# A retention and channel-mix kernel: blocks 4 and 5 in 64-token chunks, block 8 turned by transfers, and another written order

## The chip, the core and the metric

The kernel runs on one core of a Trainium2 chip, as one launch. The metric is the time of that launch on the device, in microseconds; less is better. Before the change it is 153.48 us (median of 3 runs, 153.37 to 153.55).

## What is computed

Four sequences of 768 tokens with 8 heads of 64 go through a recurrent retention: each head holds a 64 x 64 state that decays by its own factor and adds k v at each token, and the output is q times the state. The output (512 features a token) goes through a channel mix: each token is blended with the one before it, and two blends feed a squared-ReLU pair of products (512 to 1024 to 512) and a sigmoid gate.

```python
for t in range(S):
    state = gamma * state + einsum('bhd,bhe->bhde', k[:, :, t], v[:, :, t])
    y[:, :, t] = scale * einsum('bhd,bhde->bhe', q[:, :, t], state)
...
xk = mu_k * x + (1.0 - mu_k) * x_prev
xr = mu_r * x + (1.0 - mu_r) * x_prev
k = np.maximum(xk @ w_k, 0.0)
v = k * k @ w_v
r = 1.0 / (1.0 + np.exp(-(xr @ w_r)))
return (r * v).astype(np.float32)
```

Inputs and output are float32; the products run on float16.

## The kernel before

The 3072 tokens are cut into 12 blocks of 256, numbered 0 to 11, three to a sequence. A block's work is a row of steps, and each step is one function:

- `lq`, `lk`, `lv`: POOL issues transfers that bring the block's queries, keys and values into rings of four buffers, queries and keys as float16. `vs` (L291, VectorE) scales the values by the decays.
- `Tq`, `Tk`: TensorE turns queries and keys so that features lie on the partitions, and `Eq`, `Ek` (L276, ScalarE) copy them out of PSUM. A block in `PAIRQ` or `PAIRK` is turned by eight 128 x 128 transposes (L348) each, a block in neither list but in `HALF` by 32 transposes of 64 x 64 (L343), the others by L354. Blocks in `DT` are not turned by TensorE: SyncE issues a transposing transfer instead (`tq`, `tk`, L388).
- `S`: scores within a chunk. `M` (L457, VectorE): the causal mask. A block in `WIDE` has two chunks of 128 tokens, whose scores fill 128 x 2048 (L425), so it has two masks. A block in `HALF` has four chunks of 64, with half as many scores (L412) and one mask. Blocks 0 and 1 are in a third form (L433).
- `C`: the products of keys and values that carry the state from chunk to chunk (L487 wide, L469 half). `U` (L522): the sums of these, two for a wide block and four for a half one. `G`: the decay into the next block (L527 on ScalarE, L531 on VectorE).
- `I`, `J` (L544): queries times the carried state; `Y`: masked scores times values (L590 wide, L574 half; in a half block the second part of L544 follows within `Y`). `sy` is a small copy that orders the two.
- `D`: the eviction of the retention output with its scale (L640 in one piece, L633 in two for a half block). `dx` (L655): the difference from the token before. `X` (L681): the two blends, one instruction for each of four feature groups, `X.n.0.j` for the keys' blend and `X.n.1.j` for the gate's.
- `K` (L695 for a pair of blocks, L705 for one): the key products of the channel mix; `Qa`, `Qb` (L727, L741, L745; ScalarE): ReLU and square. `R` (L754) and `s` (L760): the gate and its sigmoid. `V` (L766): the value products, in two halves. `O` (L772, VectorE): the gated result; `st`: its store, issued by SyncE.

Blocks 3 and 4, 6 and 7, 9 and 10 go through `dx`, `X` and `K` as pairs, under the number of the first. `z` are products of zeros that fill TensorE while it waits at the start.

The order of all steps is written out by hand as words in one string: `S.6@67` is the score step of block 6 into PSUM banks 6 and 7, `Eq.6~a` runs on ScalarE (`v` VectorE, `p` POOL, `s` SyncE). The program is emitted word by word, and each engine runs its own words in that order; semaphores make it wait for what it needs from other engines. A bank or a buffer is used again once its last reader is done, so the bank numbers set waits too.

Of the kernel before, what the change touches and what calls it, by code (L numbers as in the profile page):

```python
# [44 lines left out]
Qb.1.2~a Tq.3@0 D.2~v R.1.1@7 s.1.0 Eq.3~a wv.0~p C.3@23 dx.2~v Tk.3@4 U.3.0~a R.0.0@5 lq.7~p
Ek.3~a U.3.1 X.2.0.1 Tk.4@2 wv.1~p X.2.0.3 s.0.1 S.3.0@01 X.2.0.2 S.3.1@34 s.0.0 lk.5~p X.2.0.0
Tq.4@6 s.1.1 M.3.0 K.2.1@5 Eq.4~a K.2.3@7 M.3.1 lq.5~p Qa.2.1~a Ek.4~a K.2.0@6 X.2.1.1 vs.4~v
Qa.2.3~a I.3@45 lv.5~p S.4.1@23 Qa.2.0~a S.4.0@01 K.2.2@7 G.3~a M.4.1 Y.3 Qb.2.0~a M.4.0 C.4@23
Qb.2.3~a V.0.1.0@6 Qa.2.2~a U.4.0~v J.3 Qb.2.2~a U.4.1 I.4@01 Y.4 sy.4~a D.3~v Qb.2.1~a lq.6~p
Tq.7@23 Qb.1.3~a J.4 V.1.1.0@7 X.2.1.3 G.4~a D.4~v V.0.0.0@4 Eq.7~a lv.7~p V.0.1.1 dx.4~v  # L50
V.1.0.0@5 dx.3~v V.0.0.1 X.2.1.0 lv.8~p V.2.1.0@2 X.3.0.0 X.3.0.1 Tk.5@3 V.1.1.1 X.2.1.2 Ek.5~a
lv.6~p X.3.0.2 V.1.0.1 X.3.0.3 Tq.5@3 X.3.1.1 K.3.5@0 lk.7~p O.0.1 V.2.1.1 O.1.1 X.3.1.2 K.3.1@1
O.1.0 K.3.2@7 lk.6~p Qa.3.1~a X.3.1.3 Eq.5~a K.3.3@5 vs.5~v Qa.3.5~a R.2.1@1 O.0.0 Qa.3.3~a
K.3.0@0 vs.7~v st.0.0 s.2.1 st.0.1 Qb.3.3~a K.3.6@3 st.1.1 X.3.1.0 Qa.3.0~a st.1.0 lv.11~p
Qa.3.2~a S.5.1@45 vs.6~v S.5.0@01 Qb.3.5~a C.5@6 K.3.4@7 Qb.3.1~a U.5.0~v lv.10~p M.5.0 Qa.3.6~a
R.3.0@6 Qb.3.0~a Qa.3.4~a R.2.0@3 M.5.1 s.3.0 lv.9~p Tq.6@01 s.2.0 I.5@67 O.2.1 Tk.6@45 sy.5~a
Eq.6~a Y.5 lq.8~p Tk.7@23 Qb.3.2~a J.5 R.3.1@0 D.5~v lq.11~p Qb.3.4~a V.2.0.0@1 Ek.7~a dx.5~v
V.2.0.1 s.3.1 Qb.3.6~a K.3.7@0 X.5.1.2 Ek.6~a lk.8~p X.5.0.1 V.3.0.0@2 vs.8~v Qa.3.7~a C.6@45
Qb.3.7~a X.5.1.1 S.6@67 lq.9~p X.5.0.2 V.3.1.0@0 U.6.0~a U.6.1 V.4.0.0@3 U.6.2 O.2.0 lq.10~p
V.3.0.1 M.6 st.2.0 R.4.0@1 U.6.3 X.5.1.0 S.7@45 s.4.0 O.3.0 I.6@67 V.4.0.1 sy.6~a G.6~a M.7 st.3.0  # L60
Tq.8@12 Y.6 X.5.1.3 Eq.8~a C.7@45 X.5.0.0 V.3.1.1 U.7.0~v lk.11~p X.5.0.3 R.5.0@1 U.7.1 U.7.2
K.5.1@2 U.7.3 lk.10~p s.5.0 D.6~v K.5.0@4 V.4.1.0@1 G.7~v Qa.5.0~a lk.9~p O.4.0 Qa.5.1~a I.7@45
O.3.1 C.8@67 sy.7~a Tk.8@23 dx.6~v st.3.1 Y.7 Ek.8~a st.2.1 V.4.1.1 D.7~v K.5.2@0 R.5.1@2 dx.7~v
Qa.5.2~a Qb.5.0~a K.5.3@3 s.5.1 X.6.0.3 R.4.1@0 Qb.5.1~a X.6.0.1 Qb.5.2~a V.5.0.0@2 tk.9~s X.6.0.2
Qa.5.3~a X.6.0.0 V.5.1.0@4 Qb.5.3~a s.4.1 vs.10~v tq.9~s K.6.4@3 K.6.7@0 X.6.1.3 Qa.6.4~a tq.10~s
X.6.1.1 V.5.0.1 Qa.6.7~a O.4.1 K.6.1@3 X.6.1.2 K.6.6@5 U.8.0~v Qa.6.1~a U.8.1 Qb.6.7~a V.5.1.1
vs.9~v K.6.2@3 U.8.2 O.5.1 I.8@67 S.8@01 Qa.6.2~a X.6.1.0 K.6.0@4 tk.11~s Qb.6.2~a M.8 Qa.6.6~a
R.6.0@3 Qa.6.0~a O.5.0 Y.8 s.6.0 S.9@45 st.5.0 Qb.6.6~a D.8~v C.9@01 st.4.1 R.7.1@3 tk.10~s
Qb.6.1~a Qb.6.0~a K.6.3@2 dx.8~v tq.11~s R.6.1@6 Qa.6.3~a X.8.1.0 s.7.1 K.6.5@7 X.8.1.3 Qb.6.3~a
st.4.0 X.8.0.1 st.5.1 R.7.0@3 Qb.6.4~a X.8.0.2 X.8.0.0 Qa.6.5~a V.7.0.0@2 X.8.0.3 U.9.0~a s.7.0  # L70
U.9.1 K.8.3@7 vs.11~v Qb.6.5~a K.8.0@3 Qa.8.3~a M.9 V.7.0.1 Qa.8.0~a X.8.1.1 K.8.2@7 Qb.8.0~a
U.9.2 U.9.3 V.6.1.0@3 O.7.0 Qa.8.2~a s.6.1 G.9~v st.7.0 C.10@01 S.10@45 Qb.8.2~a U.10.0~v I.9@67
K.8.1@2 sy.9~a M.10 V.6.1.1 Qa.8.1~a U.10.1 Qb.8.3~a U.10.2 V.6.0.0@4 U.10.3 Qb.8.1~a O.6.1
I.10@01 Y.9 sy.10~a X.8.1.2 C.11@23 G.10~v Y.10 D.9~v V.8.0.0@5 V.8.0.1 D.10~v R.8.1@6 dx.9~v
# [865 lines left out]
```

## Time and profile before

| | |
|---|---|
| median of 3 runs | 153.48 us |
| the profiled execution | 153.66 us |
| its span, first to last instruction | 151.8 us |
| TensorE matmuls busy | 143.5 us (95%) |
| VectorE busy | 127.6 us (84%) |
| ScalarE busy | 92.9 us (61%) |
| POOL busy | 62.0 us (41%) |
| granted TensorE clock | 1.000 |
| bytes read and written | 24.31 MB and 6.29 MB |

The profile is of one execution; its times are in microseconds. Rows of groups read: line, engine, operation, output and inputs with their shapes, count, then total and mean (ns) and the idle time ahead of the group with what ended it. Rows of a timeline and of the chain begin with the start and the length. In the rows of waits stand the total, the number and the longest. PE is TensorE, PEld its weight loads, DVE VectorE, ACT ScalarE, SP SyncE. The products of a row overlap, so the chain, which counts each stretch of time once, tells better than the mean of one what a product costs. Rows of the program's order carry no time.

### The profile page before, as it was taken

To read this page: it belongs to the slowest core of one execution; us is meant where nothing else is said; L and a number is where in the kernel's file an instruction comes from. 1 tells how busy PE (TensorE), PEld (TensorE's weight loads), DVE (VectorE), ACT (ScalarE), POOL (GpSimd) and SP (SyncE) were. 2 spreads that over 40 slices of the span, in tenths; PEclk is the share of its full clock that TensorE was granted. 3 is DMA by queue.
4 is the path that set the end of the run, shared out by engine and by line. 5 is a ranking of instruction groups with operands and counts; after the bars stand their busy time and mean duration, and the time that the engine had idled before them with its cause. 6 is when DMAs were issued, how large, how long until landed. Compare 5 with 4: busy or idle time off the path is not lost.

```text
span 151.8 us, 4947 instructions
## 1 busy us (share of the span) xinstructions
PE 143.5 (95%) x2125; PEld 82.6 (54%) x2125; DVE 127.6 (84%) x204; ACT 92.9 (61%) x179; POOL 62.0 (41%) x77
## 2 busy tenths in 40 slices
PE   7888789999999999999989999999999999999991
PEld 3355458757864544555457634546664444546650
DVE  2289799999999999969979999999899995399141
ACT  3665724998986229996435664778741078931860
POOL 7974678999549852997558000000000000000000
PEclk9999999999999999999999999999999999999999
DMA  4999999999999999999999947369200035000404
GB/s 137 245 236 190 181 244 242 162 171 210 196 175 239 226 208 196 322 221 186 161 219 142 210 85 139 67 178 246 73 4 0 4 140 207 0 4 29 179 33 174
DMA packets 56525, 23.83 MB, mean 157 GB/s; under 512 B 48056, under 2 KB 52024, under 8 KB 56504
## 3 DMA queue, kind: packets, MB, share of 16 engines
q0 software_dynamic: 45200, 14.95, 83.2%
q1 hardware_dynamic: 10872, 8.26, 18.1%
q8 instruction: 16, 0.26, 0.8%
q10 hardware_dynamic: 432, 0.32, 0.7%
q14 instruction: 5, 0.04, 0.1%
HBM read 24.31 MB, written 6.29 MB: 202 GB/s over the span
## 4 chain that ended last, share of the span: by engine, by line
PE 72%; DVE 10%; DMA 6%; ACT 4%; POOL 3%; issue 2%; DVEq 0%; POOLq 0%
PE ps L766 24%; PE ps L695 14%; PE ps L754 11%; PE ps L705 9%; DMA q<-in_q_dram 6%; DVE xk L681 2%; PE ps L348 2%; PE ps L544 2%; ACT k2s L745 2%; ACT kr L727 2%; PE ps L590 2%; PE ps L425 2%; DVE dx L655 2%; DVE a L457 2%; DVE xT L633 1%
## 5 line engine op out<-in xcount | busy, mean ns | idle before, releaser
L766 PE MATMUL ps<-wv,k2s 128*128 128x512 f16 x184 | 43.7, 379 | 0.0
L727 ACT ACTIVATE kr<-ps 128x512 f32<-128x512 f32 x48 | 27.6, 599 | 22.0 <-PE ps L705 12.0
L766 PEld LDWEIGHTS <-k2s 128*128 128x128 f16 x184 | 17.4, 98 | 19.3
L457 DVE TENSOR_TENSOR a<-ps,c_sb 128x1024 f16<-128x1024 f32 (+1 forms) x20 | 21.7, 1109 | 4.0 <-PE ps L412 3.2
L754 PE MATMUL ps<-wr,xr 128*128 128x512 f16 x96 | 24.0, 380 | 0.0
L760 ACT ACTIVATE rs<-ps 128x512 f32<-128x512 f32 x24 | 13.9, 598 | 15.9 <-PE ps L754 6.6
L695 PE MATMUL ps<-xk,wk 128*128 128x512 f16 x96 | 22.7, 379 | 0.1
L705 PE MATMUL ps<-xk,wk 128*128 128x256 f16 x192 | 22.8, 273 | 0.0
L270 POOL DMA_DIRECT2D v<-in_v_dram x20 | 17.9, 901 | 9.2 <-DVE vs L291 3.9
L705 PEld LDWEIGHTS <-wk 128*128 128x128 f16 x192 | 18.4, 98 | 3.7
L681 DVE SCALAR_TENSOR_TENSOR xr<-dx,mu,xT 128x256 f16<-128x256 f32 (+1 forms) x36 | 19.8, 566 | 0.1
L772 DVE SCALAR_TENSOR_TENSOR os<-ps,rs 128x512 f32<-128x512 f32 x23 | 15.3, 681 | 5.4 <-ACT rs L760 5.3
L270 POOL DMA_DIRECT2D k<-in_k_dram x20 | 17.6, 899 | 5.3 <-PE ps L469 3.1
L681 DVE SCALAR_TENSOR_TENSOR xk<-dx,mu,xT 128x256 f16<-128x256 f32 (+1 forms) x36 | 18.7, 567 | 0.1
L291 DVE TENSOR_TENSOR vs<-v,csm_sb 128x1024 f16<-128x1024 f32 x12 | 14.6, 1216 | 2.9 <-DMA v<-in_v_dram 2.9
L695 PEld LDWEIGHTS <-wk 128*128 128x128 f16 x96 | 9.1, 97 | 11.1 <-DVE xk L681 0.6
L655 DVE TENSOR_TENSOR dx<-xT 128x1024 f32<-128x1024 f32 x12 | 14.5, 1221 | 0.2
L741 ACT ACTIVATE k2s<-kr 128x512 f16<-128x512 f32 x24 | 14.5, 632 | 0.1
L745 ACT ACTIVATE k2s<-kr 128x512 f16<-128x512 f32 x24 | 14.1, 628 | 0.2
L754 PEld LDWEIGHTS <-xr 128*128 128x128 f16 x96 | 8.9, 98 | 9.3 <-DVE xr L681 0.2
L276 ACT COPY kT<-ps 128x1024 f16<-128x1024 f16 (+1 forms) x10 | 9.3, 930 | 7.1 <-PE ps L348 3.4
L270 POOL DMA_DIRECT2D q<-in_q_dram x12 | 10.7, 904 | 1.5 <-DMA v<-in_v_dram 0.7
(74 smaller groups left out, 150.4 us busy)
## 6 DMA issues: line engine op xcount, KB each, us to landing
out_dram<-os SPq DMA_DIRECT2D x23, 256.0 KB, 2.4
v<-in_v_dram POOLq DMA_DIRECT2D x20, 256.0 KB, 7.4
k<-in_k_dram POOLq DMA_DIRECT2D x21, 128.0 KB, 6.3
q<-in_q_dram POOLq DMA_DIRECT2D x13, 128.0 KB, 7.7
q<-in_q_dram POOLq DMA_DIRECT2D x5, 256.0 KB, 8.9
v<-in_v_dram POOLq DMA_DIRECT2D x2, 512.0 KB, 6.8
wv<-in_moe_w_v_dram POOLq DMA_DIRECT2D x2, 512.0 KB, 9.5
wk<-in_moe_w_k_dram POOLq DMA_DIRECT2D x2, 256.0 KB, 9.2
```

What stands on the lines that cost most here:

```text
L270: e.dma_start(out=to[:, i, hs], in_=src[:, i])
L291: e.tensor_tensor(out=VS(n), in0=V32(n).rearrange("p (h i d) -> p i h d", i=2, h=H), in1=gks[:, int(half(n) or wide(n)), :, :, None].to_br ...
L457: nc.vector.tensor_tensor(out=dst, in0=dst if n in SPLITM else src, in1=mask[:, None, None, :].to_broadcast(list(dst.shape)), op=ALU.mult,)
L655: e.tensor_tensor(out=DX(k)[:, :, m * TM + t0 : m * TM + t1], in0=x[:, :, c + t0 : c + t1], in1=x[:, :, c - 1 + t0 : c - 1 + t1], op=ALU.s ...
L681: nc.vector.scalar_tensor_tensor(out=XM[w](k)[:, j, t0:t1], in0=DX(k)[:, j, t0:t1], scalar=mu[:, w * NCO + j : w * NCO + j + 1], in1=x[:, ...
L695: nc.tensor.matmul(banks("K", n, g), lhsT=wk16[:, co, g * P : g * P + P], rhs=XM[0](k)[:, co, :], start=(co == 0), stop=(co == NCO - 1),)
L705: nc.tensor.matmul(pz[:, i, :], lhsT=wk16[:, co, fo * P : fo * P + P], rhs=XM[0](k)[:, co, m * TM + t0 : m * TM + t1], start=(i == 0 and c ...
L727: nc.scalar.activation(out=kr, in_=banks("K", n, g, *u), func=AF.Relu)
L745: nc.scalar.activation(out=K2(n)[:, w * g : w * g + w, t0:t1], in_=kr.rearrange("p a t -> p (a t)").rearrange("p (i t) -> p i t", i=w), fu ...
L754: nc.tensor.matmul(banks("R", n, tb), lhsT=XM[1](k)[:, co, t : t + P], rhs=wr16[:, co, :], start=(co == 0), stop=(co == NCO - 1),)
L766: nc.tensor.matmul(banks("V", n, tb), lhsT=K2(n)[:, fo, tb * P : tb * P + P], rhs=wv16[:, fo, :], start=(fo == 0), stop=(fo == NFO - 1),)
L772: nc.vector.scalar_tensor_tensor(out=OS(2 * n + tb), in0=banks("V", n, tb), scalar=1.0 / (KSC * KSC), in1=RS(2 * n + tb), op0=ALU.mult, op ...
```

## The change

Blocks 4 and 5 leave `WIDE`, `PAIRQ` and `PAIRK` and enter `HALF`: they are computed in 64-token chunks and turned by 64 x 64 transposes. Block 8 enters `PAIRQ` and `PAIRK` and the list of blocks turned by transposing transfers, which is now one list for queries and one for keys with the same members. Ahead of the first score products the order of words is the same but for one bank; behind them all of it is a new order, with other banks. Of that string the lines around block 1's scores are shown.

```diff
-HALF = (6, 7, 8, 9, 10, 11)
+HALF = (4, 5, 6, 7, 8, 9, 10, 11)
...
-PAIRQ = (3, 4, 5, 9, 10, 11)
-PAIRK = (3, 4, 5, 9, 10, 11)
-WIDE = (2, 3, 4, 5)
+PAIRQ = (3, 8, 9, 10, 11)
+PAIRK = (3, 8, 9, 10, 11)
+WIDE = (2, 3)
...
-DT = (9, 10, 11)
+DTQ = (8, 9, 10, 11)
+DTK = (8, 9, 10, 11)
...
-M.0.0.2.4 vs.1~v wk.0~p z.4@6 Y.0 Tk.1@2 D.0~v mt@3 C.1@45 me Ek.1~a Tq.1@3 U.1.0~v dx.0~v Tq.2@0
-Eq.1~a U.1.1 z.1@1 S.1.1@23 Eq.2~a I.1@67 X.0.0.1 S.1.0@45 lv.2~p M.1.1 G.1~a M.1.0 wr~p X.0.0.0
+M.0.0.2.4 vs.1~v wk.0~p z.4@6 Y.0 mt@0 Tk.1@1 D.0~v me C.1@45 Ek.1~a Tq.1@0 U.1.0~v dx.0~v Eq.1~a
+U.1.1 z.3@7 I.1@01 S.1.1@23 X.0.0.3 Tq.2@4 M.1.1 S.1.0@67 lv.2~p Eq.2~a M.1.0 wr~p X.0.0.0 z.5@5
...
     def laid(t, n):

-        if n in DT:
+        if n in (DTK if t is KT else DTQ):
             return t(n).rearrange("c j i p -> c (j i) p").rearrange("c (i j) p -> c j i p", j=NJ)
         return t(n)
```

More of the change, by code (lines that the diff above doesn't have):

```diff
@@ L45 @@
[L45 to L74, printed above, removed]
@@ L81 @@
[L81 to L85 removed]
+Tq.0.0.2@0 ck.0.0.2~a lq.1~p Eq.0.0.2~a lq.2~p z.3@7 Tk.0.0.2@1 Ek.0.0.2~a wk.1~p gy.1~a z.3@7
@@ new lines @@
+G.3~a Tk.4@67 M.3.0 I.3@23 K.2.3@1 sy.3~a Ek.4~a X.2.1.1 Y.3 Qa.2.2~a C.4@67 J.3 S.4@45 Qa.2.3~a
+U.4.0~v V.1.1.0@0 D.3~v Qb.2.2~a Qb.2.0~a V.0.0.0@1 lq.6~p X.2.1.0 Qb.2.3~a U.4.1 V.0.1.0@2
+Qb.2.1~a X.2.1.3 U.4.2 V.1.0.0@3 M.4 V.0.0.1 U.4.3 dx.3~v Tq.7@67 I.4@45 V.0.1.1 lq.11~p sy.4~a
+O.0.0 Y.4 st.0.0 O.0.1 V.1.0.1 D.4~v lk.6~p st.0.1 R.2.0@2 O.1.0 V.1.1.1 s.2.0 lk.7~p dx.4~v
+Eq.7~a V.2.0.0@1 O.1.1 Tk.5@23 Tq.5@67 lv.6~p X.3.0.0 Tq.6@45 R.2.1@0 X.3.0.3 Eq.6~a X.3.0.2
+V.2.0.1 Ek.5~a lv.7~p X.3.0.1 V.2.1.0@4 G.4~a vs.5~v V.2.1.1 Eq.5~a X.3.1.3 K.3.7@5 lq.10~p s.2.1
@@ new lines @@
+O.2.0 K.3.6@6 O.2.1 Qa.3.7~a X.3.1.2 C.5@01 st.2.1 Qa.3.6~a S.5@45 st.1.1 U.5.0~v Tk.6@23 st.1.0
+X.3.1.0 K.3.2@6 Ek.6~a X.3.1.1 K.3.0@7 Qb.3.7~a U.5.1 vs.6~v K.3.3@2 Qa.3.0~a Qb.3.6~a R.4.0@3
+U.5.2 lv.10~p Qa.3.3~a M.5 K.3.5@7 s.4.0 Qa.3.2~a vs.7~v I.5@23 S.6@45 lv.8~p sy.5~a C.6@01 Y.5
+M.6 U.6.0~a Qb.3.2~a K.3.4@6 Qb.3.0~a lv.9~p D.5~v R.4.1@4 Qa.3.4~a Qb.3.3~a K.3.1@5 U.6.1
+Qa.3.5~a dx.5~v lk.9~p R.3.1@2 Qa.3.1~a R.3.0@3 Qb.3.1~a U.6.2 X.5.0.0 s.3.1 lk.8~p V.3.0.0@5
+X.5.1.3 s.3.0 X.5.0.3 s.4.1 U.6.3 I.6@23 C.7@67 X.5.0.2 sy.6~a Tk.7@01 X.5.0.1 Y.6 lq.8~p vs.8~v
@@ L86 @@
+O.11.0 Vc.11.1.1@0 st.11.0 Oc.11.1.0 sc.11.1.0~s Oc.11.1.1 sc.11.1.1~a
 """
```

53 lines of the change are left out of this document (34 added, 19 removed).

## The prediction

> **What bounds the kernel now.** I read the page first, then the busy times by stage, then TensorE's waits, and last the chain and the timelines of single engines.
>
> The head of the page (busy time and share of the span), then the shares of the chain that ended last:
>
> ```profile
> span 151.8 us, 4947 instructions
> PE 143.5 (95%) x2125; PEld 82.6 (54%) x2125; DVE 127.6 (84%) x204; ACT 92.9 (61%) x179; POOL 62.0 (41%) x77
> ```
>
> ```profile
> PE 72%; DVE 10%; DMA 6%; ACT 4%; POOL 3%; issue 2%; DVEq 0%; POOLq 0%
> ```
>
> The stages (columns: length, then busy time of PE, PEld, DVE, ACT, POOL):
>
> ```profile
> 20.00:64.00 44.00, 43.47 (x564) 27.72 (x567) 43.72 (x63) 31.85 (x61) 32.92 (x39) 1.00 1.55 215
> 64.00:90.00 26.00, 25.40 (x559) 14.76 (x544) 23.57 (x38) 16.59 (x32) 14.41 (x17) 1.00 1.58 177
> 90.00:149.00 59.00, 58.60 (x751) 31.76 (x748) 47.03 (x78) 33.29 (x63) 0.00 (x0) 1.00 0.33 93
> ```
>
> TensorE is full from 20 us to its end, just short of 149 us. VectorE is full too, but only up to 90 us. So the end is the sum of TensorE's work and its waits, and until 90 us VectorE can become the bound at once. The waits of TensorE after 20 us:
>
> ```profile
> PE ps L574 <- issue: 0.5, 1, 0.5
> ...
> PE ps L590 <- ACT seen_y L276: 0.3, 1, 0.3
> PE ps L425 <- DVE xT L640: 0.2, 1, 0.2
> ```
>
> and, in the list of all engines' waits, one of the weight loads:
>
> ```profile
> PEld L695 <- DVE xk L681: 0.6, 1, 0.6
> ```
>
> That is 1.6 us. The last is that of the first key product of blocks 6 and 7 (K.6.4) for its mixed tokens; in the chain it starts here:
>
> ```profile
> 89.40 1.90 PE ps L695 x8
> ```
>
> **The change, part by part.**
>
> *TensorE's work.* The chain gives each group's time free of overlap. A block in 128-token chunks (turning, scores, state, scores times values, carried state):
>
> ```profile
> 32.81 0.24 PE ps L544 x8
> ...
> 36.25 0.45 PE ps L348 x8
> 36.70 0.55 PE ps L425 x16
> ...
> 42.19 0.57 PE ps L590 x16
> 42.76 0.25 PE ps L487 x16
> 43.01 0.97 PE ps L766 x4
> ...
> 54.23 0.86 PE ps L766 x4
> ```
>
> A block in 64-token chunks, same steps:
>
> ```profile
> 64.25 0.27 PE ps L343 x32
> ...
> 97.97 0.38 PE ps L574 x32
> 98.34 0.15 PE ps L544 x14
> 98.49 0.30 PE ps L412 x32
> 98.80 0.27 PE ps L469 x32
> ```
>
> Turning and carried state happen twice a block. Wide: 0.90 + 0.55 + 0.25 + 0.57 + 0.48 = 2.75 us. Half: 0.54 + 0.30 + 0.27 + 0.38 + 0.30 = 1.79 us. Blocks 4 and 5 save 2 x 0.96 = 1.9 us, and block 8 gives up two turnings, 0.54 us. Together **-2.45 us**, all on the path, since nothing else shortens a full engine.
>
> A switch between full-size products and small ones has a price: the four products (L766) behind a small group take 0.97 us in the rows above, elsewhere 0.86. The new order has 22 such switches from Y.1 on, the old one 20, because blocks 4 and 5 were turned by full-size transposes (L348) and are now turned in 64 x 64 tiles: **+0.2 us**.
>
> The Trainium skill, "TensorEngine Tiling (Array Packing)", Key Properties, speaks against the change here: every change of the tiling mode drains the engine. The weight loads show such a stop of 0.42 us:
>
> ```profile
> 34.39 0.33 PEld L487 LDWEIGHTS <-k 128*64 128x64 f16 x16 [0.42 <-issue]
> ```
>
> By that rule, with a full 0.42 us lost on the path at each, the two switches would cost 0.8 instead of 0.2 us; the 0.11 us between the two rows of L766 says that most of it is hidden, and I keep that.
>
> *VectorE's work.*
>
> ```profile
> L457 DVE TENSOR_TENSOR a<-ps,c_sb 128x1024 f16<-128x1024 f32 x16 | 19.1, 1215 | 4.0 <-PE ps L412 3.2 <-PE ps L433 0.8
> L522 DVE TENSOR_TENSOR tg<-ps,tg 128x256 f16<-128x256 f32 x20 | 8.4, 418 | 1.4 <-PE ps L469 1.2
> L633 DVE TENSOR_TENSOR xT<-ps,gy_sb 128x512 f32<-128x512 f32 x12 | 8.3, 690 | 2.2 <-PE ps L544 1.3
> L640 DVE TENSOR_TENSOR xT<-ps,gy_sb 128x1024 f32<-128x1024 f32 x6 | 7.3, 1220 | 1.3 <-ACT qT L276 1.1
> ```
>
> Two maskings go (-2.43), four state sums come (+1.67), two whole evictions of the retention output become four halves (+0.32): -0.44 us. So VectorE loses a fifth of what TensorE loses.
>
> *The start.* In the list of order the turning of block 2's queries (Tq.2) moves from ahead of block 1's scores (S.1.1) to between them.
>
> ```profile
> 16.05 0.79 PE L354 MATMUL ps<-c_sb,q 128*64 128x128 f16 x16 [1.20 <-DMA q<-in_q_dram]
> ...
> 17.09 0.42 PE L433 MATMUL ps<-qT,kT 64*64 64x128 f16 x16
> ...
> 31.60 0.31 PE L544 MATMUL ps<-qT,tg 64*64 64x128 f16 x8
> ```
>
> ```profile
> 14.91 1.03 ACT L276 COPY qT<-ps 128x1024 f16<-128x1024 f16 x1
> ```
>
> ```profile
> 16.36 0.47 DVE L681 SCALAR_TENSOR_TENSOR xk<-dx,mu,xT 128x256 f16<-128x256 f32 x1
> 17.63 2.36 DVE L457 TENSOR_TENSOR a<-ps,c_sb 128x1024 f16<-128x1024 f32 x2 [0.80 <-PE ps L433]
> ```
>
> S.1.1 needs ScalarE's copy, done at 15.94, not the transfer that lands at 16.0. It can start 1.1 us sooner; the masks (L457) then start when VectorE is free, 16.83 instead of 17.63, so **-0.8 us**. It is at most 1.1 and at least 0, should a later load hold the next step.
>
> *ScalarE and SyncE.* Block 8 gives up two evictions, each like the copy above (1.03 us), and gets two transfers instead:
>
> ```profile
> kT<-k SPq DMA_TRANSPOSE x3, 3.2
> qT<-q SPq DMA_TRANSPOSE x3, 3.2
> ```
>
> ScalarE loses 2.1 us, but is 61% busy; I count nothing. The transfers stand on SyncE's queue behind the stores of block 3 and ahead of those of block 4. Block 8's loads are issued, by the count of loads below, twelve issues of 0.9 us behind vs.6 (some 61.5 us), and land 7.1 to 11.1 us later, at 79 to 83 us; the two transfers then end by 90. Its scores come four groups into blocks 6 and 7, about 92 us. If that cover went, TensorE would wait for the excess. Behind the transfers wait the stores of blocks 4 and 5, whose tiles come up for reuse only with the results of blocks 6 and 7: nothing.
>
> *New waits.* Two masks took 2.36, so they follow each other at 1.14; short mixes (L681) follow at 0.40. With such spacings I went along the new order, engine by engine, to the places where one needs another.
>
> VectorE's row around block 2's second masks as it was (a_2 masked scores, tg_2_95 the first sum of its state, vs_76 its scaled values, xr_105 block 1's gate mixes; the first masks stand ahead of these rows):
>
> ```order
> L291 TENSOR_TENSOR vs_76<-v_2_72,csm_sb 128x1024
> L681 SCALAR_TENSOR_TENSOR xr_104<-dx_99,mu,xT_130 128x256
> L681 SCALAR_TENSOR_TENSOR xr_105<-dx_100,mu,xT_130 128x256 x2
> L522 TENSOR_TENSOR tg_2_95<-ps,tg_2_89 128x256
> L457 TENSOR_TENSOR a_2_85<-ps,c_sb 128x1024
> L291 TENSOR_TENSOR vs_74<-v_3_73,csm_sb 128x1024
> ```
>
> The same place on VectorE now:
>
> ```order
> L291 TENSOR_TENSOR vs_76<-v_2_72,csm_sb 128x1024
> L681 SCALAR_TENSOR_TENSOR xr_105<-dx_100,mu,xT_130 128x256 x2
> L457 TENSOR_TENSOR a_2_85<-ps,c_sb 128x1024
> L522 TENSOR_TENSOR tg_2_95<-ps,tg_2_89 128x256
> L681 SCALAR_TENSOR_TENSOR xr_105<-dx_100,mu,xT_130 128x256
> L291 TENSOR_TENSOR vs_74<-v_3_73,csm_sb 128x1024
> ```
>
> Both masks now stand ahead of the sum, for which block 2's inter product (I.2) waits. From 16.83 VectorE does five masks and value scalings (5.7), D.1 and dx.1 (2.3) and 13 mixes (5.2), then the sum (0.34): 30.4 us. TensorE started I.2 at 31.60; now one gate group less (0.86) stands ahead of it, and it comes 0.8 sooner, so it gets there at 29.9: a wait of 0.5 us (0 to 1).
>
> ScalarE's row around block 4's keys (kT_81 their copy, qT_78 that of its queries, tg_1_88 the state carried into block 4) as it was:
>
> ```order
> L276 COPY qT_78<-ps 128x1024
> L727 ACTIVATE kr_110<-ps 128x512
> L276 COPY kT_81<-ps 128x1024
> L727 ACTIVATE kr_107<-ps 128x512
> L727 ACTIVATE kr_108<-ps 128x512
> L527 ACTIVATE tg_1_88<-t_0_86,csm_sb 128x64 x4
> ```
>
> The same place on ScalarE now:
>
> ```order
> L276 COPY qT_78<-ps 128x2x4x128
> L727 ACTIVATE kr_109<-ps 128x512
> L745 ACTIVATE k2s<-kr_107 128x512
> L727 ACTIVATE kr_110<-ps 128x512
> L527 ACTIVATE tg_1_88<-t_0_86,csm_sb 128x64 x4
> L276 COPY seen_y<-ps 128x4
> L276 COPY kT_81<-ps 128x2x8x64
> ```
>
> The keys' copy now stands behind the four carried-state steps, and block 4's state products share its banks (6 and 7), so they wait for it; VectorE's first sum waits for them, where two masks stood before. The four steps cost:
>
> ```profile
> 41.09 1.08 ACT L527 ACTIVATE tg<-t,csm_sb 128x64 f16<-128x64 f32 x4
> ```
>
> VectorE's wait lies between 0 and these steps plus a copy, 2.1 us; I take the middle, 1.1 us, and 0.25 us on TensorE, which has other products ready.
>
> POOL's row of loads from block 7's values on as it was (v_3_73 holds block 7's values, v_0_70 block 8's, v_2_72 block 6's and then 10's, v_1_71 block 9's):
>
> ```order
> L270 DMA v_3_73<-in_v_dram 128x8x64 x2
> L270 DMA v_0_70<-in_v_dram 128x8x64 x2
> L270 DMA v_2_72<-in_v_dram 128x8x64 x2
> L270 DMA k_3_69<-in_k_dram 128x8x64 x2
> L270 DMA k_2_68<-in_k_dram 128x8x64 x2
> ```
>
> POOL's row from block 6's values on now:
>
> ```order
> L270 DMA v_2_72<-in_v_dram 128x8x64 x2
> L270 DMA v_3_73<-in_v_dram 128x8x64 x2
> L270 DMA q_2_64<-in_q_dram 128x8x64 x2
> L270 DMA v_2_72<-in_v_dram 128x8x64 x2
> L270 DMA v_0_70<-in_v_dram 128x8x64 x2
> L270 DMA v_1_71<-in_v_dram 128x8x64 x2
> ```
>
> Block 8's values now queue behind block 10's, which must wait until block 6's are scaled (vs.6). The rows that price this:
>
> ```profile
> 59.93 5.32 POOL L270 DMA_DIRECT2D v<-in_v_dram x6 [3.93 <-DVE vs L291]
> ...
> DMA to landing us min/median/max: 5.7/7.1/11.1
> ```
>
> Block 8's last piece is issued 3 x 0.89 = 2.7 us after vs.6 and lands 9.8 us after it. VectorE does 9.3 us of work between vs.6 and vs.8 (two masks, vs.7, D.5, dx.5, four sums, five mixes): a wait of 0.5 us, which reaches TensorE at block 5's key product behind D.6. Bounds: none (5.7) and 4.5 us (11.1).
>
> Smaller ones, 0.1 to 0.3 us each, stand at the scores of block 2, the first key products (weights landing), block 2's second inter product, and the gate of block 4: 1.2 us. New waits of TensorE together 0.5 + 0.25 + 0.5 + 1.2 = 2.45 us, where 1.6 go: **+0.85 us**.
>
> *The sum.* -2.45 + 0.2 - 0.8 + 0.85 = -2.2 us. The profiled execution took 153.66 us, 151.8 of it the span; it becomes 151.5 us. The median of the runs shown, 153.48, is 0.18 us lower: **151.3 us**.
>
> **The rivals.**
>
> *VectorE takes over.* By the same count VectorE has 68.8 us of work from block 1's masks to the mixes that K.6.4 needs, where it had 68.0, and starts 0.8 us sooner: so without new waits K.6.4 comes no later than now, and two value products of block 5 (1.7 us) now stand ahead of it instead of behind. If all of VectorE's new waits, 1.1 us behind block 4's keys and 0.5 us for block 8's values, come on top of all that it waits now, K.6.4 starts 1.6 us late, of which the 1.7 us make good just about all: 153.4 us. If half of them do: **152.5 us**. For it: 43.72 of 44 us busy. Against it: of its 2.4 us of waits from 64 to 90 us, 1.1 were for ScalarE's copies (L640) and most of 1.2 for TensorE's state products (L522), both of which come sooner.
>
> *The values of block 8 come late (slower).* One load at the slow end, 11.1 us, holds VectorE for 4.5 us, and D.6, block 5's products and blocks 6 and 7 behind it: 151.3 + 4.0 = 155.3 us. It decides from a landing 2.2 us later than the median. For it: at 60 us the load queue had already run dry once for 3.93 us. Against: the 11.1 us stand where the queue was full; here it is nearly empty.
>
> *Nothing comes of it.* The order is packed for other durations than the chip's, and small waits add up to the 2.2 us: 153.5 us. That the change fails to remove work is excluded by the count of instructions.
>
> **How the numbers follow.** Forecast (150.1 to 152.2): 0.58. VectorE takes over (152.2 to 153.4): 0.18. No change: 0.08. Late values: 0.16. A difference under 0.2%, 0.3 us, can't be told from none by this kernel's runs. The low end is the forecast with no more waits than now and without the 0.2 us of switches, 151.3 - 1.05, and 0.15 of the start's open 0.3 us: 150.1. The high end takes in nearly all of the second case: 153.2. Faster is 0.58 and 0.16 of the second case, 0.74; same 0.02 of that and 0.08, 0.10; slower 0.16.
>
> **What would show it.** In the profile after: L343 x256, L348 x16, L457 x14, L522 x24, four transfers each for q and k; S.1.1 near 16.0 and the masks near 16.8; TensorE over 97% busy from 20 us to its end, some 2.2 us sooner than now. Wrong would be: VectorE idle for over 1.5 us ahead of a scaling of values (L291), TensorE idle for more than 3 us after 20 us, or K.6.4 later than 89.4.

## The result, and the profile after

The changed kernel takes 154.54 us (median of 20 runs, 153.46 to 156.33), the kernel before 153.91 us beside it (20 runs, 153.37 to 155.22): a ratio of 1.0048, 95% interval 1.0026 to 1.0070. It is a little slower, where 151.3 us was forecast, and the range from 150.1 to 153.2 doesn't hold it. Ratios and intervals, here and below, leave out the few runs that took over 1.5% more than the fastest of their kernel, while medians are over all runs. The profiled execution of the changed kernel took 153.46 us, the shortest of its twenty; a second one, of the same kernel, is used below for a usual run (155.34 us, "the second profile").

The head of the page after, the shares of its chain, and a group that changed (count, busy time and mean, then idle time ahead and what ended it):

```profile
span 151.7 us, 5268 instructions
PE 142.4 (94%) x2285; PEld 81.1 (53%) x2285; DVE 126.7 (84%) x208; ACT 90.5 (60%) x176; POOL 61.2 (40%) x76
...
PE 63%; DMA 15%; DVE 12%; issue 4%; POOL 3%; ACT 0%; DVEq 0%; POOLq 0%
...
L772 DVE SCALAR_TENSOR_TENSOR os<-ps,rs 128x512 f32<-128x512 f32 x23 | 15.4, 685 | 6.7 <-DMA out_dram<-os 4.7
```

TensorE does less work, but with 160 products and as many weight loads more. The idle time of VectorE ahead of the results (L772) now ends with a store. Before, it ended with ScalarE's sigmoid:

```profile
L772 DVE SCALAR_TENSOR_TENSOR os<-ps,rs 128x512 f32<-128x512 f32 x23 | 15.3, 681 | 5.4 <-ACT rs L760 5.3
```

The stretch from block 1's scores times values (Y.1) to TensorE's last product, by the busy times by stage (length, then busy time of PE, PEld, DVE, ACT, POOL). The row of the kernel before:

```profile
20.04:148.60 128.56, 127.47 (x1848) 74.24 (x1847) 113.92 (x175) 81.73 (x155) 47.29 (x55) 1.00 1.00 151
```

The same stretch in the changed kernel's first profile:

```profile
19.09:147.36 128.27, 126.07 (x2008) 72.67 (x2007) 112.71 (x178) 80.17 (x156) 47.07 (x55) 1.00 1.05 156
```

And in its second profile:

```profile
19.55:148.82 129.27, 126.20 (x2008) 72.47 (x2007) 112.25 (x178) 80.05 (x156) 47.63 (x56) 1.00 1.03 155
```

These rows and the spans give the whole difference, term by term, in us against the profile before:

| | forecast | first profile | second profile |
|---|---|---|---|
| Y.1 starts sooner | -0.8 | -0.95 | -0.49 |
| TensorE's work after it (busy) | -2.25 | -1.40 | -1.27 |
| TensorE's waits after it (length less busy) | +0.85 | +1.11 | +1.98 |
| from TensorE's end to the end of the span | 0 | +1.14 | +1.55 |
| sum | -2.2 | -0.1 | +1.8 |

The last term is 3.19 us before (148.60 to 151.79), 4.33 (147.36 to 151.69) and 4.74 (148.82 to 153.56) after. So the start came; the work shrank by less than forecast; in the first profile waits and the end took back all but 0.1 us of both, in the second more than all.

The longest new wait was ended by no engine, transfer or buffer that the profile shows. TensorE's timeline in the first profile around the state products of block 6 (C.6, L469), which stand between block 5's inter product and its scores times values (L574):

```profile
64.64 0.45 PE L412 MATMUL ps<-qT,kT 64*64 64x64 f16 x32
64.89 0.22 PE L469 MATMUL ps<-vs,k 64*64 64x64 f16 x4
65.82 0.41 PE L469 MATMUL ps<-vs,k 64*64 64x64 f16 x28 [0.70 <-issue]
66.06 0.49 PE L574 MATMUL ps<-a,vs 64*64 64x64 f16 x32
```

It stops after 4 of 32 like products and waits for nothing that the profile shows ("issue"). The keys had landed at 57.1, the values were scaled at 63.1 us. What arrives in that moment is in the list of DMA queues, for 63.3 to 64.4 us (packets, MB, share of 16 engines):

```profile
q1 hardware_dynamic: 187, 0.34, 83.1%
q0 software_dynamic: 168, 0.02, 29.6%
q8 instruction: 1, 0.02, 5.4%
```

The one packet of the queue q8 is 16 KB of TensorE's own instructions, fetched between 63.40 and 64.34 us. That row of the whole page, for the kernel before:

```profile
q8 instruction: 16, 0.26, 0.8%
```

For the changed kernel, two packets more:

```profile
q8 instruction: 18, 0.29, 0.8%
```

### The profile page after: what moved, and what is told of

Its sections match the earlier page's. It is cut to its first block, busy times and chain, and to the rows that moved or that the text cites. A ratio compares the mean times of both kernels' runs of the same rounds, so it can differ in the third digit from the quotient of the medians.

```text
span 151.7 us, 5268 instructions
## 1 busy us (share of the span) xinstructions
PE 142.4 (94%) x2285; PEld 81.1 (53%) x2285; DVE 126.7 (84%) x208; ACT 90.5 (60%) x176; POOL 61.2 (40%) x76
## 4 chain that ended last, share of the span: by engine, by line
PE 63%; DMA 15%; DVE 12%; issue 4%; POOL 3%; ACT 0%; DVEq 0%; POOLq 0%
PE ps L766 23%; PE ps L695 11%; PE ps L754 10%; DMA v<-in_v_dram 10%; PE ps L705 9%; DMA wk<-in_moe_w_k_dram 5%; DVE dx L655 2%; DVE xk L681 2%; PE ps L544 2%; PE ps L469 2%; DVE a L457 2%; PE ps L574 2%; PE ps L343 1%; PE ps L412 1%; DVE xr L681 1%
## 5 line engine op out<-in xcount | busy, mean ns | idle before, releaser
L766 PE MATMUL ps<-wv,k2s 128*128 128x512 f16 x184 | 43.0, 379 | 0.0
L727 ACT ACTIVATE kr<-ps 128x512 f32<-128x512 f32 x48 | 28.1, 596 | 22.8 <-PE ps L695 12.9
L754 PE MATMUL ps<-wr,xr 128*128 128x512 f16 x96 | 23.4, 379 | 0.0
L457 DVE TENSOR_TENSOR a<-ps,c_sb 128x1024 f16<-128x1024 f32 (+1 forms) x18 | 19.5, 1099 | 3.7 <-PE ps L412 3.6
L772 DVE SCALAR_TENSOR_TENSOR os<-ps,rs 128x512 f32<-128x512 f32 x23 | 15.4, 685 | 6.7 <-DMA out_dram<-os 4.7
L633 DVE TENSOR_TENSOR xT<-ps,gy_sb 128x512 f32<-128x512 f32 x16 | 11.0, 689 | 2.3 <-PE ps L544 1.2
L270 POOL DMA_DIRECT2D q<-in_q_dram x10 | 9.0, 921 | 7.1 <-PE ps L343 6.8
```

Of the source, the lines that this page charges most:

```text
L270: e.dma_start(out=to[:, i, hs], in_=src[:, i])
L457: nc.vector.tensor_tensor(out=dst, in0=dst if n in SPLITM else src, in1=mask[:, None, None, :].to_broadcast(list(dst.shape)), op=ALU.mult,)
L727: nc.scalar.activation(out=kr, in_=banks("K", n, g, *u), func=AF.Relu)
L754: nc.tensor.matmul(banks("R", n, tb), lhsT=XM[1](k)[:, co, t : t + P], rhs=wr16[:, co, :], start=(co == 0), stop=(co == NCO - 1),)
L766: nc.tensor.matmul(banks("V", n, tb), lhsT=K2(n)[:, fo, tb * P : tb * P + P], rhs=wv16[:, fo, :], start=(fo == 0), stop=(fo == NFO - 1),)
L772: nc.vector.scalar_tensor_tensor(out=OS(2 * n + tb), in0=banks("V", n, tb), scalar=1.0 / (KSC * KSC), in1=RS(2 * n + tb), op0=ALU.mult, op ...
```

## The experiments

Kernels of one set ran on one chip, beside runs of the kernel before; ratios are to these.

**First: the end, and the parts alone in the old order.** The end of the changed kernel:

```diff
- ... st.9.1 st.9.0 ... st.10.1 ... st.10.0     (all behind O.9.1)
+ O.10.1 st.10.1 O.10.0 st.10.0 ... O.9.0 st.9.0 ... O.9.1 st.9.1
```

> The changed kernel with one edit: SyncE issues the last four whole stores in the order in which their results are done (10.1, 10.0, 9.0, 9.1) instead of all behind 9.1. Theory (the tail): in the changed kernel block 11's first result waits until 146.77 us for the landing of a store, though its products are done near 145.5. With the edit it starts near 145.5, the last stores leave sooner, and the execution is 0.9 us shorter than the changed kernel's, so within 0.2% of the kernel before. Rival: the last value products (done near 147.2) set the end anyway; then 0.3 us or less comes of it. Up to 139 us this run is also a second profile of the changed kernel: if its typical time is about 1 us above that of its first profile because block 8's turning transfers land late, the inter product of block 8 waits for them here.

Measured: 153.81 us, ratio 1.0005 (0.9977 to 1.0033); the profiled execution 154.30 us. Its tail answers one question, VectorE's timeline (lines are one lower in this kernel):

```profile
142.44 0.69 DVE L771 SCALAR_TENSOR_TENSOR os<-ps,rs 128x512 f32<-128x512 f32 x1 [0.91 <-ACT kr L726]
146.76 0.69 DVE L771 SCALAR_TENSOR_TENSOR os<-ps,rs 128x512 f32<-128x512 f32 x1 [3.63 <-PE ps L765]
147.65 0.42 DVE L790 SCALAR_TENSOR_TENSOR os<-ps,rs 128x256 f32<-128x256 f32 x1 [0.19 <-PE ps L783]
148.45 0.42 DVE L790 SCALAR_TENSOR_TENSOR os<-ps,rs 128x256 f32<-128x256 f32 x1 [0.38 <-PE ps L783]
```

Block 11's first result now waits for TensorE and no store, and the ratio is within the 0.2% that was expected. But the profiles show little of the 0.9 us at the end: 4.1 us lie behind TensorE's last product, where the first profile had 4.3. Its middle answers the other question. To 60 us TensorE is within 0.3 us of the first profile; then the same stop comes at the same product, and longer, in TensorE's timeline:

```profile
64.94 0.24 PE L468 MATMUL ps<-vs,k 64*64 64x64 f16 x4
66.81 0.41 PE L468 MATMUL ps<-vs,k 64*64 64x64 f16 x28 [1.64 <-issue]
67.06 0.49 PE L573 MATMUL ps<-a,vs 64*64 64x64 f16 x32
```

The 16 KB packet came between 64.41 and 65.36 us, 1.0 us later than in the first profile, and TensorE went on 1.0 us later. So the guess in the expectation, that block 8's transfers cost the usual run its time, is not borne out here: from 67 us to the last value products this execution keeps its 1.0 us and adds none.

The start alone, in the kernel before:

```diff
- Tq.2@0 Eq.1~a U.1.1 z.1@1 S.1.1@23 Eq.2~a
+ Eq.1~a U.1.1 z.1@1 S.1.1@23 Tq.2@0 Eq.2~a
```

> The kernel before with the start's edit alone: the turning of block 2's queries goes behind block 1's first scores. The prediction's step: the masks of block 1 start at 16.8 instead of 17.6 us and the end comes 0.8 us sooner (ratio 0.995). Rival: loads that land at 22 to 30 us (key weights, values of blocks 2 and 3) set the next step; then the masks start sooner but the gain is gone by block 2's values: 0.2 us or less at the end.

Measured: ratio 0.9985 (0.9958 to 1.0011), unclear. The interval does not hold the 0.995 of the prediction's step; the rival's 0.2 us or less fits. In its profile Y.1 starts 0.69 us sooner (19.35); block 2's scores then stop for 0.5 us (0.1 before), and the stop near 76 us is 1.0 us (0.6 before), both without a releaser. At 77 us nothing is left of the gain.

Blocks 4 and 5 as half blocks alone, in the old order:

```diff
-HALF = (6, 7, 8, 9, 10, 11)
+HALF = (4, 5, 6, 7, 8, 9, 10, 11)
-WIDE = (2, 3, 4, 5)
+WIDE = (2, 3)
- S.4.1@23 ... S.4.0@01 ... M.4.1 ... M.4.0 ... U.4.1 I.4@01 Y.4 sy.4~a ... J.4
+ S.4@01 ... M.4 ... U.4.1 U.4.2 U.4.3 I.4@01 sy.4~a Y.4     (block 5 alike; sy.3~a ahead of Y.3; C.5 in banks 0 and 1, not 6)
```

> The kernel before with blocks 4 and 5 in 64-token chunks in the old order, their turning left as it was (full-size transposes). The prediction's step: 0.6 us a block less on TensorE (scores 0.25, inter products 0.18, scores times values 0.19, less 0.02 for the state), so 1.2 us sooner (ratio 0.992). Rival: VectorE, nearly full up to 90 us, becomes the bound and TensorE waits for it what it saves: 0.5 us or less (ratio over 0.997).

Measured: 157.96 us, ratio 1.0231 (1.0175 to 1.0287). Both theories miss it: it is far slower. Its profiled execution is 3.8 us longer than that of the kernel before (spans of 155.6 and 151.8 us), and TensorE's longest stops in the list of waits are again without a releaser:

```profile
PE ps L411 <- issue: 1.7, 1, 1.7
...
PE ps L573 <- issue: 1.2, 1, 1.2
...
PE ps L342 <- issue: 1.0, 1, 1.0
```

These three come to some 4 us (4.4 us in the table below, which has them by another measure), about the time lost.

Block 8 alone turned by transfers, in the old order:

```diff
- Tq.8@12 Eq.8~a ... Tk.8@23 Ek.8~a
+ tq.8~s (behind st.3.0) ... tk.8~s (behind st.2.1)     (8 in PAIRQ, PAIRK, DT)
```

> The kernel before with block 8 alone turned by transposing transfers in the old order. The prediction's step: 0.54 us less on TensorE, nothing waits for the transfers: 0.5 us sooner (ratio 0.9965). Rival: the transfers share the DMA engines with the last loads, land near 92 us instead of by 90, and block 8's inter product waits for them in some executions: no gain, or up to 1 us slower.

Measured: 155.95 us, ratio 1.0126 (1.0078 to 1.0173), slower than either case. Block 8's inter product starts at 95.7 us, behind the landing at 92.25, and doesn't wait for it; but block 9's scores do wait for block 9's transfer, which stands behind (landed 99.64, scores at 99.78, 1.1 us idle), and a stop of 1.4 us without a releaser has come up at 83 us.

**What the stops have in common.** Number all records of TensorE in the order of their starts, from 0: products, weight loads and the dozen instructions of its sequencer. Behind 20 us, every wait of its products over 0.3 us that the profiles give as "issue" sits at a row 194 + 256 n (to within one row), in all kernels of this study, and TensorE goes on 1.2 to 1.7 us after a 16 KB packet of q8 has landed. From the records of the traces, in us (the stop is what the gap has over the usual spacing):

| kernel | row | the 256 rows ahead begun at | packet landed | went on | stop |
|---|---|---|---|---|---|
| before | 2242 | 70.3 | 75.2 | 76.7 | 0.6 |
| changed, first profile | 2242 | 59.4 | 64.3 | 65.8 | 0.9 |
| changed, stores reordered | 2242 | 59.5 | 65.4 | 66.8 | 1.8 |
| changed, second profile | 2242 | 59.8 | 64.9 | 66.2 | 0.9 |
| changed, second profile | 2754 | 72.6 | 77.5 | 78.9 | 0.8 |
| blocks 4, 5 half, old order | 1474 | 42.0 | 45.5 | 46.8 | 1.2 |
| blocks 4, 5 half, old order | 1986 | 62.1 | 66.2 | 67.6 | 1.4 |
| blocks 4, 5 half, old order | 2242 | 67.6 | 73.3 | 74.9 | 1.8 |

So TensorE's code comes in pages of 256 instructions (16 KB), and the packet with the next page starts about when one begins: up to 3.4 us before that where full-size products stand in line, up to 5.0 us after it while the loads run; it takes 0.9 to 2.0 us. A page of 128 full-size products (1.73 us for 8) would last nearly 28 us; one that is mostly small products is through in 4 to 6, and then TensorE waits for its code. That the queue is TensorE's follows from the counts: each profile has exactly as many 16 KB packets as its program has such rows (16, 17 or 18, in programs of 4134 to 4582 records), and none of the 257 pages of the 16 profiles was begun sooner than 1.2 us after its packet had landed. The Trainium skill, "Runtime: NRT & Kernel Launch", section on instruction fetch mechanics, states such pages of 16 KiB and 256 instructions, fetched by a DMA queue while the page ahead runs, at a cost that is mostly hidden. The runs agree on the size and the order of fetching; the cost here is up to 1.8 us at one page.

**Second: pages as cause.** The kernel before with the same work, its pages cut elsewhere. `y.48` is 48 products of zeros, 64 x 64:

```diff
- Eq.0.0.2~a lq.2~p z.3@7
+ Eq.0.0.2~a lq.2~p z.1@7 y.48@7
```

> The kernel before with its work and order unchanged, but two of the filling products of zeros at the start (0.43 us) are replaced by 48 small ones (64 x 64, about the same time), which are 92 instructions more on TensorE. Theory (code pages): TensorE's instructions come in pages of 256, each asked for when the page ahead of it begins and usable 3.5 to 7.3 us later; a page used up sooner makes TensorE wait without any semaphore. In the kernel before only one page is (0.67 us near 76 us). The shift by 92 cuts the same row elsewhere, so that several pages between 58 and 98 us hold almost only small products: 4 to 7 us slower in all, in stops at pages' first rows. Rival (no such thing; the stops without a semaphore belong to the steps): within 0.3 us of the kernel before.

Measured: 157.55 us, ratio 1.0235 (1.0187 to 1.0283): 3.5 us slower than the kernel before for work that is the same, a little less than the 4 to 7 us expected. TensorE's timeline near 85 us, where the kernel before has no stop:

```profile
84.29 0.44 PE L573 MATMUL ps<-a,vs 64*64 64x64 f16 x32
84.55 0.25 PE L543 MATMUL ps<-qT,tg 64*64 64x64 f16 x6
86.25 0.28 PE L543 MATMUL ps<-qT,tg 64*64 64x64 f16 x10 [1.45 <-issue]
```

It has four stops of 0.9 to 1.6 us at pages' first rows (at 21, 69, 81 and 86 us), 4.4 us in all, where the kernel before has 0.7. The difference is about the time lost.

Fewer instructions for more work, in the changed kernel:

```diff
-PAIRK = (3, 8, 9, 10, 11)
+PAIRK = (3, 5, 6, 7, 8, 9, 10, 11)
- Tk.5@23 ... Tk.6@23 ... Tk.7@01
+ Tk.5@2 ... Tk.6@2 ... Tk.7@0
```

> The changed kernel with the keys of blocks 5, 6 and 7 turned by 8 full-size transposes each instead of 32 small ones: 0.18 us more work each, 0.54 us in all, but 144 instructions less on TensorE between 52 and 73 us. Theory (code pages): the stop of 0.9 to 1.9 us ahead of block 5's masked scores times values shrinks to 0.3 us or less, and no other grows by as much: 0.5 to 1.5 us faster than the changed kernel. Rival (work alone counts): 0.5 us slower than it.

Measured: 152.88 us, ratio 0.9939 (0.9910 to 0.9968), beside 154.47 us of the changed kernel on the same chip: 1.6 us faster with more work. In the profiles a part of that is pages, whose stops behind Y.1 hold TensorE for 0.4 us where they held it for 0.9 in the first profile of the changed kernel and 1.6 in the second. A part is the end: 3.65 us behind TensorE's last product, against 4.33 and 4.74. The same place in its timeline of TensorE:

```profile
65.45 0.47 PE L468 MATMUL ps<-vs,k 64*64 64x64 f16 x32
65.74 0.37 PE L573 MATMUL ps<-a,vs 64*64 64x64 f16 x20
66.35 0.29 PE L573 MATMUL ps<-a,vs 64*64 64x64 f16 x12 [0.24 <-issue]
```

Less traffic on the DMA engines:

```diff
- lq.11~p ... lq.10~p ... lk.9~p ... lk.10~p ... lq.9~p ... lk.11~p
```

> The changed kernel without the twelve transfers that load the queries and keys of blocks 9, 10 and 11 (those blocks use what lies in the buffers). TensorE's instructions are the same. Theory (pages wait behind loads on the DMA engines): with fewer packets between 48 and 82 us each page comes sooner, the page that TensorE waits for near 65 us is there in under 5 us from its request, and the stop at that place goes from 0.9 or 1.8 to under 0.4 us. Rival (the delay of a page is fixed): the stop stays at 0.9 us or more.

This kernel leaves out twelve loads and takes what lies in the buffers for the queries and keys of blocks 9 to 11; it has one execution, of 153.89 us. The page of row 2242 landed 2.8 us after the page ahead began (5.0 in the first profile), and there is no stop. But the page of row 1730 came 5.3 us after the one ahead began (2.2 in the first profile), with a stop of 0.9 us at 54 us, where only the first of the missing loads had been due. The time at the end did not fall. That loads delay pages is borne out at one place; the run settles no more.

The changed kernel once more:

> The changed kernel once more, for a third profile of it and for its time beside the runs above. Theory: what its profiled execution takes above the 153.46 us of the first profile is, within 0.4 us, what the stop ahead of block 5's masked scores times values is longer than 0.9 us (and the one ahead of block 2's scores longer than 0.3). Rival: the stops are as in the first profile and the time is lost elsewhere.

Measured: 154.47 us, ratio 1.0041 (1.0004 to 1.0077), the profiled execution 155.34 us. 1.9 us more than the first profile, but the stop at row 2242 is the same 0.9 us. The theory misses the place; less than half of it is at another page, row 2754, ahead of the second half of block 3's value products:

```profile
76.32 1.80 PE L705 MATMUL ps<-xk,wk 128*128 128x256 f16 x15
78.89 1.47 PE L766 MATMUL ps<-wv,k2s 128*128 128x512 f16 x6 [0.77 <-issue]
```

0.5 us more are lost at the start (Y.1 at 19.55) and 0.4 us at the end.

**Third: do the losses add up?** Fewer instructions and a mended end, the mended end alone, and one more turning by full-size transposes:

```diff
 (both) the stores' order of the first experiment, and
- sc.11.1.0~s Oc.11.1.1 sc.11.1.1~a
+ sc.11.1.0~a Oc.11.1.1 sc.11.1.1~s
 (first) PAIRK and banks as in the kernel with fewer instructions
```

> The changed kernel with the keys of blocks 5, 6 and 7 turned by full-size transposes (as in the run with fewer instructions) and with its end mended: the last four whole stores in the order of their results, and the very last store issued by SyncE instead of ScalarE. Theory: page stops and the end are separate losses and add up: 0.6% faster than the kernel before by the first, another 0.4 to 0.6% by the second, so a ratio near 0.989. Rival: the end is set by something both share; then no better than 0.994.

> The changed kernel with its end mended alone. In the changed kernel 4.3 us lie between TensorE's last product and the end of the span (3.2 in the kernel before): the first result of block 11 waits for a store to land (0.35 us of it at the end), the last store lands 0.4 us later after its issue, and after it SyncE clears seven more semaphores one after the other (0.45 us), because its wait for ScalarE's store stands first in its list. Theory: 3.2 to 3.5 us remain, 0.8 to 1.1 us faster than the changed kernel, ratio to the kernel before 0.997 to 0.999. Rival: only the wait for the store counts: 0.3 us, ratio 1.002.

```diff
 the kernel with fewer instructions, and
-PAIRQ = (3, 8, 9, 10, 11)
+PAIRQ = (3, 5, 8, 9, 10, 11)
- Tq.5@67
+ Tq.5@6
```

> The changed kernel with the keys of blocks 5, 6 and 7 and now also the queries of block 5 turned by full-size transposes: 48 instructions fewer still, 0.18 us more work than the run with fewer instructions. Theory (code pages): what counts is where the rows of 256 are cut. The page that TensorE begins near 66 us would now reach from block 5's scores times values past the scores of block 6 into the turning and state of later blocks and lasts under 4 us without stops; worked out with pages usable 5.7 to 6.4 us after their request near there, a stop of 3 to 4 us appears in this stretch, and the run is 2 to 4 us slower than the one with fewer instructions. Rival (fewer instructions are better, or only work counts): 0.2 us from it.

Measured: both 153.58 us, 0.9993 (0.9958 to 1.0028); the end alone 153.84 us, 1.0001 (0.9968 to 1.0033); one more turning 153.57 us, 0.9977 (0.9941 to 1.0014). The first theory fails: nothing adds up to 0.989. The end alone is 0.4% nearer to the kernel before than the changed kernel was, less than forecast, and its profile shows why: the last result follows TensorE by 0.46 us as in the kernel before, but 1.9 us lie between the last landing and the end of the span (1.4 in the changed kernel, 1.0 in the kernel before), so that 4.1 us remain behind TensorE's last product (3.2 to 3.5 expected). The third forecast fails too: the page that was to be usable 5.7 us or more after the one ahead of it began was usable after 3.0, and the stop was 0.8 us instead of 3 to 4. Where a page is cut can be counted; how late it comes can't be told from another run.

**Fourth: luck or cause, and the queue of the last store.**

> The kernel with fewer instructions once more (keys of blocks 5, 6 and 7 turned by full-size transposes), for a second set of times. Theory: what it gained is the page stops, so it stays faster than the kernel before by 0.2 to 0.7%, and each stop without a semaphore sits at a multiple of 256 rows. Rival: the first set was luck, as the run with the mended end (0.9993) suggests; then a ratio of 0.998 to 1.001.

Measured: 153.31 us, 0.9973 (0.9943 to 1.0003). The stop at row 2242 is 1.1 us in its profiled execution, against 0.4 in the first set. By the ratios it is faster than the changed kernel (1.0041 and 1.0048) in both sets; against the kernel before the second set alone can't tell it from none.

```diff
 the kernel before
- sc.11.1.1~a Oc.11.1.0 sc.11.1.0~s
+ sc.11.1.1~s Oc.11.1.0 sc.11.1.0~a
```

> The kernel before with one edit at its end: the very last store is issued by ScalarE and the one ahead of it by SyncE, as in the changed kernel. Theory: SyncE waits for ScalarE's store first and clears the other semaphores after it, so 0.45 us more lie between the last landing and the end of the span (1.0 becomes 1.4): ratio 1.003. Rival: the end does not depend on the queue: ratio 1.000 and 1.0 us.

Measured: ratio 1.0021 (0.9988 to 1.0054), unclear; but the profile has 3.23 us behind TensorE's last product, against 3.19. The queue of the last store costs nothing, so that half of the theory falls. The other half, SyncE's list, was not varied here: the last store kept its semaphore. In the records SyncE goes through the semaphores of the landings at the end in one fixed order (106, 107, 109, 111, 112, 114 to 117), some 0.06 us for each once they have landed. Before, and in this run, the last store has 116, the last but one of the list. In the changed kernel it has 107, the second, and seven more follow: the list takes 0.55 us from there instead of 0.15. It has 107 in the kernel with block 8's transfers alone too, where two more transfers shift all that follows them by two semaphores. This is 0.4 us of the end: 1.4 us from the last landing to the end of the span in both, 1.0 before.

```diff
-PAIRQ = (3, 8, 9, 10, 11)        -PAIRK = (3, 8, 9, 10, 11)
+PAIRQ = (3, 5, 8, 9, 10, 11)     +PAIRK = (3, 5, 7, 8, 9, 10, 11)
- Tk.5@23 Tq.5@67 ... Tk.7@01
+ Tk.5@2 Tq.5@6 ... Tk.7@0
```

> The changed kernel with the keys and queries of block 5 and the keys of block 7 turned by full-size transposes: as much work and as many instructions as the kernel with fewer instructions, but the pages between 53 and 60 us are cut 48 rows apart from its. Theory: the stop ahead of block 5's scores times values is 0.1 to 0.8 us, no other one over 0.4 us behind 30 us, and it is 0.3 to 0.9% faster than the changed kernel. Rival (more work, no gain): 0.3% slower than it.

Measured: 153.34 us, 0.9974 (0.9943 to 1.0004), with a stop of 0.9 us at row 2242 (0.1 to 0.8 expected) and none over 0.3 us behind 30 us otherwise. Against the changed kernel's ratios that is 0.7% faster, as the theory said.

**What the end of the changed kernel waits for.** With the same order of stores, the changed kernel's last whole stores take 3.9 to 4.2 us to land, those of the kernel with fewer instructions 2.0 to 2.4. From the view of one source line (the stores, 141 to 147 us), the changed kernel:

```profile
DMA to landing us min/median/max: 3.9/4.0/4.2
```

The same in the kernel with fewer instructions:

```profile
DMA to landing us min/median/max: 2.0/2.2/2.4
```

Between 142 and 147 us the changed kernel's list of DMA queues has one packet that the other's has not:

```profile
q1 hardware_dynamic: 570, 1.04, 55.4%
q8 instruction: 1, 0.02, 1.8%
```

It is the 18th page, at 143.13 us, 1.4 us long. In the three profiles of this order of stores with a page among them the stores take about 4 us; in the four without (fewer instructions twice, the two other cuts) about 2. Other orders agree: where a page comes among the stores (block 8's transfers alone, and one store each in the two kernels with reordered stores and the changed kernel's instructions) it is 3.6 to 4.4 us, and 2.0 in the kernel with reordered stores and fewer instructions, which has no page there. No run varied the page alone. On this hangs VectorE's wait in the first profile's timeline:

```profile
141.39 0.69 DVE L772 SCALAR_TENSOR_TENSOR os<-ps,rs 128x512 f32<-128x512 f32 x1 [0.91 <-ACT kr L727]
146.77 0.69 DVE L772 SCALAR_TENSOR_TENSOR os<-ps,rs 128x512 f32<-128x512 f32 x1 [4.69 <-DMA out_dram<-os]
147.38 0.75 DVE L791 SCALAR_TENSOR_TENSOR os<-ps,rs 128x256 f32<-128x256 f32 x2
```

Block 11's first result takes the buffer of block 9's first, whose store landed at 146.64; its products were done at 145.6.

## Why the prediction was wrong, point by point

No single step carries the miss. Against the forecast, in the first and the second profile, the work missed by +0.85 and +0.98 us, the waits by +0.26 and +1.13, the end by +1.14 and +1.55 and the start by -0.15 and +0.31: 2.1 and 4.0 us in all. The end, put at nothing without a reason, is the largest in both.

- *The start, -0.8 us: right, and not kept.* Block 1's scores (S.1.1) and masks in the timelines of TensorE and VectorE after:

```profile
16.05 0.42 PE L433 MATMUL ps<-qT,kT 64*64 64x128 f16 x16
```

```profile
16.69 2.35 DVE L457 TENSOR_TENSOR a<-ps,c_sb 128x1024 f16<-128x1024 f32 x2
```

  Y.1 came 0.95 us sooner in the first profile, 0.49 in the second. Alone in the old order the gain was gone by 77 us, in two page stops.
- *TensorE's work, -2.45 + 0.2 us: right in sign, mis-sized.* It measured -1.40 and -1.27. By the time from one product's start to the next, less idle time, the wide steps gave 5.4 us in the first profile, as priced (5.5), and the full-size products grew by 0.4 (0.2 was priced for the switches). The small products that took the wide steps' place cost 3.65 us, where 3.04 was priced. The prices of a half block's steps were taken from groups that follow other small ones. Block 4's stand alone between full-size products, in the chain:

```profile
40.19 0.37 PE ps L343 x32
...
42.22 0.38 PE ps L469 x32
```

  0.37 and 0.38 us, against the 0.27 that was used for each. The Trainium skill, "TensorEngine Tiling (Array Packing)", Key Properties, states that changing the tiling mode drains TensorE. By that rule the prediction had 0.8 us for two switches, so -1.65 in all. This came nearer in total than the 0.2 us that was kept, though not by its own term: the full-size products grew by 0.4 us, and the rest is small groups that cost more standing alone.
- *Other waits, +0.85 us: named one by one with fair success, and one resource left out.* The inter product I.2 waited 0.4 us for VectorE's sum (0.5), VectorE behind block 4's keys 1.2 us (1.1), TensorE then not at all (0.25). Block 8's values brought none (0.5): they landed at 72.20, VectorE reached them at 72.34. What is missing in the sum is TensorE's instructions. By idle time, page stops behind Y.1 hold TensorE for 0.5 us before, 0.9 in the first profile, 1.6 in the second and 2.0 in the one with other stores; all other waits are 0.6 before and 1.3 to 1.4 in those three. So of the new waits that the prediction named (2.45 us) at most 1.3 us came, and of those that it let go (1.6 us) at most 1.1 were there to go. That the first profile comes within 0.3 us of the +0.85 is luck: two errors that offset each other, and a term that was not in the sum. The prediction also took the 0.5 us at L574 "<- issue" for a wait that the change removes; it was such a page, inside a row of 32 like products in the timeline before:

```profile
75.99 0.20 PE L574 MATMUL ps<-a,vs 64*64 64x64 f16 x4
76.66 0.41 PE L574 MATMUL ps<-a,vs 64*64 64x64 f16 x28 [0.47 <-issue]
```

- *The end, 0 us: the step that failed by most.* The span behind TensorE's end was carried over from before. It grew by 1.14 us in the first profile: the last result is 0.30 us later behind TensorE (0.76 against 0.46), for the buffer above; the last store takes 0.42 us longer from its result to its landing (2.15 against 1.73); SyncE's list takes 0.42 us longer. In the second profile it is 0.72, 0.42 and 0.42. With fewer instructions the first two are gone and the list stays (3.65 us in all); with block 8's transfers alone the end is 3.6 us too. In the three kernels with reordered stores SyncE pauses some 0.45 us more ahead of the last entry of its list, with all landed; why is open. That a page is why the stores land late rests on their coming together.
- *Transfers of block 8, nothing: right, barely.* They landed at 91.0 and 92.3 us instead of by 90, and the inter product came at 92.96.
- *VectorE takes over: no.* K.6.4 started at 89.41, as before. *The values late: no.* *Nothing comes of it, 153.5 us:* nearest in what it says of the change, no difference where 0.6 us was measured, but for another reason than small waits of a packed order.
- *What would show it:* L343 x256, L348 x16, L457 x14 and L522 x24 are there. TensorE was 98.3% busy (126.07 of 128.27), but ended 1.2 us sooner instead of 2.2, and in the second profile its waits behind Y.1 (3.07 us, length less busy) just passed the 3 us that were named as wrong.

Shown by experiment: that the stops sit at pages and cost time with the work unchanged (3.5 us). With fewer instructions the changed kernel is faster with more work; the profiles put this down to shorter page stops and a shorter end. Shown by the records alone: SyncE's list at the end. Only argued: how much of the 0.6 us between the medians is pages and how much the end, since the stops differ from execution to execution. A version with the same chunks that beats the changed kernel was found: its keys of blocks 5, 6 and 7 turned by full-size transposes, 0.9939 and 0.9973 of the kernel before. Against the kernel before its gain is shown in one set of two. Why the same TensorE program with a mended end measured 0.9993 is explained by half at most: its profile has 4.1 us behind TensorE's last product, against 3.65 with the stores in the old order.

## What to carry to other kernels

A cut into smaller products saves TensorE's time and spends its instructions: count both, and price a small group that stands alone between full-size ones by such a group. Where TensorE stops inside a row of like products and nothing released it, look for a packet of its instruction queue that landed some 1.4 us ahead of its going on; if there is one, look for fewer instructions in that stretch, which is what helped here, rather than for another order of the steps. And a difference of some tenths of a per cent between two orders can come from where their pages are cut. The end is a term of its own, too: two transfers more gave the last store another place in SyncE's closing list, and 0.4 us were spent there.
